# Transposing the attention probabilities by a DMA through DRAM in an attention and MLP kernel

## The chip, the cores and the metric

The kernel runs on one core of one Trainium2 chip. A core has TensorE (PE in the profile; PEld is its weight load), VectorE (DVE), ScalarE (ACT), GpSimd (POOL) and SyncE (SP), each with an instruction queue of its own that is worked through in order, an on-chip memory SBUF of 128 partitions, and the accumulation memory PSUM. Transfers are issued by SyncE and ScalarE and run on 16 DMA engines. The metric is device time in microseconds (us) for one execution, the median of several runs. Before the change it is 1058.22 us over three runs (1056.92 to 1058.27).

## The reference

Attention with a sliding window and a few global tokens, and then a two-layer MLP. Cut to what matters:

```python
# batch 8, heads 8, 512 local and 32 global tokens, head size 64, window 32
s_g  = scale * q_g @ k_all.T                        # 32 global queries see all 544 keys
out_g = softmax(s_g) @ v_all
s_ll = where(|i - j| <= 32, scale * q_l @ k_l.T, -1e9)
s_lg = scale * q_l @ k_g.T
a_l  = softmax(concat([s_lg, s_ll]))                # local queries: 32 global keys and the band
out_l = a_l @ concat([v_g, v_l])
x = concat([out_g, out_l]) as (4608 tokens, 512)
h = x @ w_in                                        # 512 -> 2048
result = (h * sigmoid(h)) @ w_out                   # 2048 -> 512
```

All is float32. The softmax divides by its sum plus 1e-9.

## The kernel before

The work is laid out as 128 attention steps (k = 0 to 127), each for one batch element, 128 local queries and a pair of heads (u = 0, 1), and as an MLP over 12 blocks of tokens (the first of 128 tokens, the rest of 384). For each block and each of 16 slices of the hidden layer, `first_layer` runs 12 matmuls (L600) and an activation chain over ScalarE and VectorE (L606, L608, L612, L613), and `second_layer` runs three matmuls for each 128 tokens (L628 to L630). Float32 accuracy comes from products of high and low parts: a tensor is rounded to the one-pass type `fp32r` (`hi`), and the rest is kept as `lo`.

The order on TensorE is the order of the program, written out by hand: every part of an attention step is put on a stream with a due time, counted in steps, and `fill` advances that stream as MLP matmuls are issued. The due times of the parts stand in `DUE`: `load=-1.2, split=-0.5, vload=-0.6, vsplit=0.95, turn=1.6, out=2.2`, relative to the step's scores. The order on the other engines and on the DMA queues is made by a planner that simulates the program; each engine then keeps to that order.

One step from k = 16 on goes like this. `st_load` and `st_vload` fetch queries with keys (`raw`) and values (`vraw`). `st_split` and `st_vsplit` make high and low parts (L320 to L322, L330, L331). `st_scores` runs the score matmuls (L350), adds the mask with a row minimum on VectorE (L354), takes the exponential on ScalarE (L358), and divides by the sum: head 0 on ScalarE (L362), head 1 on VectorE (L363). The probabilities, [128 queries, 2 heads, 256 columns, of which 224 are used] in float32, lie in `probs`. A DMA on SyncE's queue (L370) copies them to `rr`, a tile of type `fp32r`. `st_turn` transposes `rr` in four blocks of 128 x 128 on TensorE into the PSUM tile `t` (L385), ScalarE rounds `t` to `pt_hi` (L406), and VectorE makes `pt_lo` (L407); GpSimd puts the global part beside it (L409, L410). `st_out` multiplies by the values (L452 with `pt_hi`, L454 with `pt_lo`), and the results go by way of `xs` (L460, L461) into the MLP's input `xh`, `xl` (L462, L463) and into the sum `acc` (L465, L467). `pt_hi` and `pt_lo` are single tiles, so the turn of a step waits for the output matmuls of the step before. Steps below k = 16 transpose `probs` itself in full float32 (L383).

Weights are unpacked and split in the first sixth of the run (`join_weights`, `split_weights`; L211 is the split's part on GpSimd).

Of the kernel before, what the change touches and what calls it, by code (L numbers as in the profile page):

```python
# [20 lines left out]
P = 128  # L21
# [3 lines left out]
W = 224  # L25
# [10 lines left out]


SIZES = (1,) + (3,) * 11
BUFS = dict(qk=2, raw=2, p=2, vraw=2, rr=1)
ND = 28  # L40
KF = 16
GF = 3
KP = 12
# [6 lines left out]
             gload=(1.2, 2.2, 3.2, 3.3), gscores=(3.4, 4.2, 5.1, 6.0), gsoft=(4.4, 6.2), gturn=(6.9, 8.0),  # L50
             join=(3.9, 5.0, 5.9, 6.8), late=8.5, then=7.3)

DUE = dict(load=-1.2, split=-0.5, vload=-0.6, vsplit=0.95, turn=1.6, out=2.2)
HEAD = dict(load=-0.2, split=0.45, scores=0.65, soft=0.85, slot=0.3)
HEADS0, HEADS = (10, 1), (7, 2)
TURN = (1.15, 2.15)
# [4 lines left out]
def attention_moe_kernel(ctx: ExitStack, tc: tile.TileContext, qk0_in, qk_in, v_in, gqk, wts, out):  # L61
    nc = tc.nc

    const = ctx.enter_context(tc.tile_pool(name="const", bufs=1))
    raws = ctx.enter_context(tc.tile_pool(name="raws", bufs=BUFS["raw"]))
    work = ctx.enter_context(tc.tile_pool(name="work", bufs=1))
    two = ctx.enter_context(tc.tile_pool(name="two", bufs=2))
    small = ctx.enter_context(tc.tile_pool(name="small", bufs=4))
    ps_att = ctx.enter_context(tc.tile_pool(name="ps_att", bufs=1, space=PSUM))
    ps_h = ctx.enter_context(tc.tile_pool(name="ps_h", bufs=2, space=PSUM))  # L70
    ps_out = ctx.enter_context(tc.tile_pool(name="ps_out", bufs=1, space=PSUM))
# [19 lines left out]
    ident = const.tile([P, P], F32R, name="ident")  # L91
# [16 lines left out]
    mask_of = [masks[0]] + [masks[1]] * (NC - 2) + [masks[2]]  # L108
# [6 lines left out]
        return const.tile([P, 2 * DM], dtype, tag=f"wh{i}", name=name)  # L115


    probs = [const.tile([P, 2, 2 * P], F32, name=f"probs{i}") for i in range(BUFS["p"])]
    more = [scratch(SCRATCH - 1 - i, F32, f"probs{i}_") for i in range(2)]
    probs += [more[i // 2][:, DM * (i % 2) : DM * (i % 2 + 1)].rearrange("p (u j) -> p u j", u=2) for i in range(3)]  # L120
    for t in probs:
        nc.gpsimd.memset(t, 0.0)
    pgs = [const.tile([P, SKV], F32, name=f"pg{i}") for i in range(2)]

    pts = []
# [9 lines left out]
        return work.tile([P, 2, 2, P + SG], F32, tag="pt_lo" if k % 2 else "pt_hi", name=f"pt{k}")  # L135

    def probs_tile(k):
        i = k % (len(probs) if k < KP else BUFS["p"])
        held_by[i] = k
        return probs[i]  # L140

    held_by = {}

# [14 lines left out]
    def qk_tiles(name):  # L158
        return (work.tile([P, QW + KW], F32R, tag="qk", bufs=BUFS["qk"], name=f"qk{name}"),
                work.tile([P, SKV], F32R, tag="klo", bufs=BUFS["qk"], name=f"klo{name}"))  # L160

    def rr_tile(k):
        return work.tile([P, 4 * P], F32R, tag="rr", bufs=BUFS["rr"], name=f"rr{k}")

    w_32, w_hi, w_lo, w_raw, w_next = [], [], [], [], [0, 0]
# [11 lines left out]
    def join_weights():  # L179
# [81 lines left out]
    def g_soft(b, hh):  # L261
# [32 lines left out]
    tiles = {}  # L294
# [40 lines left out]
    def st_scores(k, b, c, pr):  # L335
        if k < ND:
            raw = tiles.pop(("raw", k))
        else:
            qk, klo = tiles.pop(("qk", k))
        s = attbank("s", f"s{k}")  # L340
        for u in range(2):
            o = s[:, u * W : (u + 1) * W]
            qs = slice(u * P, (u + 1) * P)
            if k < ND:
                terms = [(raw[:, qs], raw[:, QW : QW + W])]
            else:
                ks = slice(u * W, (u + 1) * W)
                terms = [(qk[:, qs], qk[:, QW:][:, ks]), (qk[:, qs], klo[:, ks])]
            for i, (q, kt) in enumerate(terms):
                nc.tensor.matmul(o, q, kt, start=(i == 0), stop=(i == len(terms) - 1))  # L350
        p = probs_tile(k)
        st = small.tile([P, 8], F32, tag="st", name=f"st{k}")
        for u in range(2):
            nc.vector.tensor_tensor_reduce(out=p[:, u, :W], in0=s[:, u * W : (u + 1) * W], in1=mask_of[c],  # L354
                                           scale=-SCALE, scalar=3.0e38, op0=ALU.add, op1=ALU.min,
                                           accum_out=st[:, u : u + 1])
        for u in range(2):
            nc.scalar.activation(p[:, u, :W], p[:, u, :W], AF.Exp, bias=st[:, u : u + 1], scale=-1.0,  # L358
                                 accum_out=st[:, 2 + u : 3 + u])
        nc.vector.tensor_scalar(out=st[:, 4:6], in0=st[:, 2:4], scalar1=1e-9, scalar2=None, op0=ALU.add)  # L360
        nc.vector.reciprocal(out=st[:, 6:8], in_=st[:, 4:6])
        nc.scalar.activation(p[:, 0, :W], p[:, 0, :W], AF.Copy, scale=st[:, 6:7])  # L362
        nc.vector.tensor_scalar(out=p[:, 1, :W], in0=p[:, 1, :W], scalar1=st[:, 7:8], scalar2=None,  # L363
                                op0=ALU.mult)
        if k < KF:
            tiles["p", k] = p.rearrange("p u j -> p (u j)")
            return

        rr = rr_tile(k)
        nc.sync.dma_start(out=rr.bitcast(F32), in_=p.rearrange("p u j -> p (u j)"))  # L370
        tiles["rr", k] = rr

    def st_turn(k, b, c, pr):
        whole = k < KF
        t = attbank("t", f"t{k}")
        if whole:
            p = tiles.pop(("p", k))
            assert k in held_by.values()
        else:
            rr = tiles.pop(("rr", k))  # L380
        for i in range(4):
            if whole:
                nc.tensor.transpose(t[:, i * P : (i + 1) * P], p[:, i * P : (i + 1) * P], ident.bitcast(F32))  # L383
                continue
            nc.tensor.transpose(t[:, i * P : (i + 1) * P].bitcast(F32R), rr[:, i * P : (i + 1) * P], ident)  # L385
        t4 = t.rearrange("p (u a q) -> p u a q", u=2, a=2)
        if k < NPR:

            pt = tiles["pt", k] = pt_whole(k)
            nc.scalar.copy(out=pt[:, :, :, :P], in_=t4)  # L390
            return
        did(("last", b) if (c, pr) == (NC - 1, NPR - 1) else k, ("turn", b, pr // 2))
        pgt, pgh, pgl = state["pgt"]
        g = pgt[:, c, 2 * pr : 2 * pr + 2, :]
        if whole:
            pt = tiles["pt", k] = pt_whole(k)
            nc.scalar.copy(out=pt[:, :, :, :P], in_=t4)
            nc.gpsimd.tensor_copy(out=pt[:, :, 0, P:], in_=g)
            if c == NC - 1:
                rows = slice(SG * pr, SG * (pr + 1))  # L400
                hi, lo = (part.bitcast(F32)[rows, :].rearrange("p (u q) -> p u q", u=2) for part in (pgh, pgl))
                nc.gpsimd.memset(pt[:, :, 1, P:], 0.0)
                nc.gpsimd.tensor_tensor(out=pt[:SG, :, 1, P:], in0=hi, in1=lo, op=ALU.add)
            return
        pt_hi, pt_lo = pt_tiles(k)
        nc.scalar.copy(out=pt_hi[:, :, :, :P], in_=t4)  # L406
        nc.vector.tensor_tensor(out=pt_lo[:, :, :, :P], in0=t4, in1=pt_hi[:, :, :, :P].bitcast(F32),  # L407
                                op=ALU.subtract)
        nc.gpsimd.tensor_copy(out=pt_hi[:, :, 0, P:], in_=g)  # L409
        nc.gpsimd.tensor_tensor(out=pt_lo[:, :, 0, P:], in0=g, in1=pt_hi[:, :, 0, P:].bitcast(F32),  # L410
                                op=ALU.subtract)
        if c == NC - 1:
            for pt, part in ((pt_hi, pgh), (pt_lo, pgl)):
                src = part[SG * pr : SG * (pr + 1), :].rearrange("p (u q) -> p u q", u=2)
                nc.gpsimd.tensor_copy(out=pt[:SG, :, 1, P:], in_=src)
# [99 lines left out]
    for k, (t, b, c, pr) in enumerate(steps):  # L515
        a = (k, b, c, pr)
        j = k % NST
# [47 lines left out]
    ends, t = [], 0  # L565
# [168 lines left out]
```

## Time and profile before

| | |
|---|---|
| runs | 1056.92, 1058.27, 1058.22 us, median 1058.22 |
| span of the profiled execution | 1057.0 us, mean granted TensorE clock 0.993 |
| TensorE busy | 1024.4 us (97%), 6128 matmuls |
| VectorE, ScalarE, GpSimd busy | 757.8 (72%), 732.6 (69%), 187.4 us (18%) |
| DMA | 126.01 MB, mean 119 GB/s; 33.1% of the 16 engines' time on SyncE's queue |
| `rr` | 112 transfers of 256 KB, 2.3 us from issue to landing |

The profiled execution is one execution; its span, from the first to the last instruction, is all the page has of its time, and lies within the times of the runs. In the rows, a group of instructions is named by line, engine and operation, then output and inputs; `x448` is their number, and behind the bar stand the busy time in us and the mean length of one in ns. Matmuls overlap, so what one costs is the distance from its start to the next one's start, not its length. In a timeline row the first number is the start in us, the second the length.

### The profile page before, as it was taken

To read this page: it belongs to the slowest core of one execution; us is meant where nothing else is said; L and a number is where in the kernel's file an instruction comes from. 1 tells how busy PE (TensorE), PEld (TensorE's weight loads), DVE (VectorE), ACT (ScalarE), POOL (GpSimd) and SP (SyncE) were. 2 spreads that over 40 slices of the span, in tenths; PEclk is the share of its full clock that TensorE was granted. 3 is DMA by queue.
4 is the path that set the end of the run, shared out by engine and by line. 5 is a ranking of instruction groups with operands and counts; after the bars stand their busy time and mean duration, and the time that the engine had idled before them with its cause. 6 is when DMAs were issued, how large, how long until landed. Compare 5 with 4: busy or idle time off the path is not lost.

```text
span 1057.0 us, 19736 instructions
## 1 busy us (share of the span) xinstructions
PE 1024.4 (97%) x6128; PEld 915.2 (87%) x6128; DVE 757.8 (72%) x2297; ACT 732.6 (69%) x1965; POOL 187.4 (18%) x480
## 2 busy tenths in 40 slices
PE   6898989999999999999999999999999999999998
PEld 4666878899898898899998898899999989999996
DVE  4877747787788878876668887887887877664322
ACT  6778867777786777776568777777777877654322
POOL 2015755111111111111001111111111111110000
PEclk8999999999999999999999999999999999999999
DMA  8894222433343343442234334344333433300000
GB/s 300 289 345 153 91 76 82 159 115 98 113 148 122 112 135 110 126 129 74 82 96 145 100 113 134 120 126 134 114 115 112 141 115 115 114 34 20 31 1 31
DMA packets 67305, 126.01 MB, mean 119 GB/s; under 512 B 7552, under 2 KB 27520, under 8 KB 67200
## 3 DMA queue, kind: packets, MB, share of 16 engines
q1 hardware_dynamic: 63456, 111.11, 33.1%
q10 hardware_dynamic: 3744, 13.63, 3.6%
q8 instruction: 49, 0.80, 0.3%
q14 instruction: 56, 0.46, 0.1%
HBM read 86.44 MB, written 8.91 MB: 90 GB/s over the span
## 4 chain that ended last, share of the span: by engine, by line
PE 78%; DVE 9%; ACT 8%; issue 3%; DMA 2%; SPq 1%; POOL 0%; ACTq 0%; DVEq 0%
PE h L600 31%; PE out L628 10%; PE out L630 10%; PE out L629 10%; PE s L350 5%; PE o L452 4%; PE o L454 3%; PE t L385 3%; ACT probs L358 2%; DVE pt_lo L407 1%; ACT t L606 1%; PE gs L245 1%; DVE w L200 1%; DVE t L608 1%; ACT w_hi L210 1%
## 5 line engine op out<-in xcount | busy, mean ns | idle before, releaser
L600 PE MATMUL h<-xh,w_hi 128*128 128x384 f32 x704 | 240.6, 342 | 0.0
L600 PE MATMUL h<-xl,w_hi 128*128 128x384 f32 x704 | 238.2, 338 | 0.0
L600 PE MATMUL h<-xh,w_lo 128*128 128x384 f32 x704 | 237.8, 338 | 0.0
L628 PE MATMUL out<-w_hi,gh 128*128 128x512 f32 x528 | 219.2, 415 | 0.0
L630 PE MATMUL out<-w_hi,gl 128*128 128x512 f32 x528 | 209.0, 396 | 0.3 <-DVE gl L613 0.3
L629 PE MATMUL out<-w_lo,gh 128*128 128x512 f32 x528 | 208.2, 394 | 0.0
L606 ACT ACTIVATE t<-h 128x384 f32<-128x384 f32 (+1 forms) x192 | 90.7, 472 | 146.6 <-PE h L600 139.8
L608 DVE SCALAR_TENSOR_TENSOR t<-t,h 128x384 f32<-128x384 f32 x176 | 97.2, 552 | 103.5 <-ACT t L606 102.2
L600 PEld LDWEIGHTS h<-xl,w_hi 128*128 128x128 f32 x704 | 132.5, 188 | 6.0 <-DVE xl L463 0.7
L600 PEld LDWEIGHTS h<-xh,w_hi 128*128 128x128 f32 x704 | 132.5, 188 | 5.2
L600 PEld LDWEIGHTS h<-xh,w_lo 128*128 128x128 f32 x704 | 132.3, 188 | 0.0
L613 DVE TENSOR_TENSOR gl<-t,gh 128x384 fp32r<-128x384 f32 x176 | 100.4, 570 | 43.0 <-PE out L630 39.0
L358 ACT ACTIVATE probs<-probs,st 128x224 f32<-128x224 f32 x244 | 115.7, 476 | 14.4 <-DVE st L354 13.3
L630 PEld LDWEIGHTS out<-w_hi,gl 128*128 128x128 f32 x528 | 99.5, 188 | 23.8 <-DVE gl L613 0.7
L409 POOL CAST pt_hi<-pgt 128x64 fp32r<-128x64 f32 x112 | 34.7, 310 | 473.8 <-PE o L454 336.1
L354 DVE CUSTOM_DVE_ANT_0 probs<-s,mask 128x224 f32<-128x224 f32 x244 | 85.4, 385 | 38.0 <-PE s L350 32.8
L628 PEld LDWEIGHTS out<-w_hi,gh 128*128 128x128 f32 x528 | 99.9, 189 | 12.4 <-issue 1.7
L629 PEld LDWEIGHTS out<-w_lo,gh 128*128 128x128 f32 x528 | 100.3, 190 | 10.8
L612 ACT CAST gh<-t 128x384 fp32r<-128x384 f32 x176 | 89.9, 511 | 26.1 <-DVE t L608 22.6
L452 PE MATMUL o<-pt_hi,vv 128*128 128x160 f32 x448 | 89.1, 266 | 2.6 <-DVE pg L251 1.7
L461 DVE TENSOR_TENSOR xs<-o,xs 64x160 f32<-64x160 f32 x224 | 70.6, 315 | 28.1 <-ACT xs L460 23.8
L452 PEld LDWEIGHTS o<-pt_hi,vv 128*128 128x128 f32 x448 | 82.5, 189 | 9.2 <-issue 5.3
(120 smaller groups left out, 1850.9 us busy)
## 6 DMA issues: line engine op xcount, KB each, us to landing
raw<-in_qk_dram SPq DMA_DIRECT2D x100, 352.0 KB, 3.0
rr<-probs SPq DMA_DIRECT2D x112, 256.0 KB, 2.3
vraw<-in_v_dram SPq DMA_DIRECT2D x128, 128.0 KB, 2.3
raw_w<-in_wts_dram ACTq DMA_DIRECT2D x26, 512.0 KB, 6.3
raw_g<-in_gqk_dram SPq DMA_DIRECT2D x32, 304.0 KB, 2.8
out_dram<-o SPq DMA_DIRECT2D x31, 256.0 KB, 2.5
raw<-in_qk_dram SPq DMA_DIRECT2D x28, 240.0 KB, 4.2
raw_w<-in_wts_dram SPq DMA_DIRECT2D x6, 512.0 KB, 7.0
```

The source lines that it names most:

```text
L354: nc.vector.tensor_tensor_reduce(out=p[:, u, :W], in0=s[:, u * W : (u + 1) * W], in1=mask_of[c], scale=-SCALE, scalar=3.0e38, op0=ALU.add, ...
L358: nc.scalar.activation(p[:, u, :W], p[:, u, :W], AF.Exp, bias=st[:, u : u + 1], scale=-1.0, accum_out=st[:, 2 + u : 3 + u])
L452: nc.tensor.matmul(o[:, at], vv[:, a, u].rearrange("p t d -> p (t d)"), pt_hi[:, u, a, :m], start=(a == 0), stop=(a == 1))
L461: nc.vector.tensor_tensor(out=xs[rows, :], in0=o[:D, at], in1=xs[rows, :], op=ALU.add)
L600: nc.tensor.matmul(h[:, :nt], wt, x[:, c, :nt], start=(i == 0), stop=(i == 3 * NCC - 1))
L606: nc.scalar.activation(t[:, :nt], h[:, :nt], AF.Tanh, scale=0.5)
L608: nc.vector.scalar_tensor_tensor(out=out[:, :nt], in0=t[:, :nt], scalar=1.0, in1=h[:, :nt], op0=ALU.add, op1=ALU.mult)
L612: nc.scalar.copy(out=gh[:, :nt], in_=t[:, :nt])
L613: nc.vector.tensor_tensor(out=gl[:, :nt], in0=t[:, :nt], in1=gh[:, :nt].bitcast(F32), op=ALU.subtract)
L628: nc.tensor.matmul(o, gh[:, sl], wh, start=(f == 0), stop=False)
L629: nc.tensor.matmul(o, gh[:, sl], wl, start=False, stop=False)
L630: nc.tensor.matmul(o, gl[:, sl], wh, start=False, stop=(f == NF - 1))
```

## The change

For steps from k = 16 on, the probabilities are seen as 16 bit halves. GpSimd copies each head's into a tile `halves`, low and high halves apart; a DMA writes `halves` into a DRAM tile `away` (two of them in turn); a transposing DMA reads `away` as a matrix of 256 rows (query, half) by 512 columns and writes its transpose into the SBUF tile `turned`, which read as float32 is the transposed probabilities. `pt_hi` and `pt_lo` are then made from `turned` instead of from the PSUM tile. The TensorE transposes of these steps, `rr` and its DMA are gone. The probabilities of these steps rotate over three half tiles instead of two whole ones, `vraw` has one buffer instead of two, and three due times move: `vload` from -0.6 to 0.2, `turn` from 1.6 to 1.7, `out` from 2.2 to 2.4. For the steps below k = 16 the tiles named `halves` and `turned` serve as probability tiles.

```diff
-BUFS = dict(qk=2, raw=2, p=2, vraw=2, rr=1)
+BUFS = dict(qk=2, raw=2, p=2, vraw=1)
...
-DUE = dict(load=-1.2, split=-0.5, vload=-0.6, vsplit=0.95, turn=1.6, out=2.2)
+DUE = dict(load=-1.2, split=-0.5, vload=0.2, vsplit=0.95, turn=1.7, out=2.4)
...
+    planes = ctx.enter_context(tc.tile_pool(name="planes", bufs=2, space=bass.MemoryType.DRAM))
...
-    probs = [const.tile([P, 2, 2 * P], F32, name=f"probs{i}") for i in range(BUFS["p"])]
+    probs = [const.tile([P, 2, 2 * P], F32, name="probs0")]
+    probs += [work.tile([P, 2, 2 * P], F32, tag=tag, name=f"probs_{tag}") for tag in ("turned", "halves")]
...
-    for t in probs:
+    third = const.tile([P, 2 * P], F32, name="third")
+    for t in probs + [third]:
         nc.gpsimd.memset(t, 0.0)
+    heads = [probs[0][:, 0], probs[0][:, 1], third]
...
     def probs_tile(k):
-        i = k % (len(probs) if k < KP else BUFS["p"])
+        if k >= KF:
+            return [heads[(2 * (k - KF) + u) % 3] for u in range(2)]
+        i = k % (len(probs) - 1 if k < KP else BUFS["p"])
         held_by[i] = k
-        return probs[i]
+        return [probs[i][:, u] for u in range(2)]
...
         if k < KF:
-            tiles["p", k] = p.rearrange("p u j -> p (u j)")
+            tiles["p", k] = p
             return
-
-        rr = rr_tile(k)
-        nc.sync.dma_start(out=rr.bitcast(F32), in_=p.rearrange("p u j -> p (u j)"))
-        tiles["rr", k] = rr
+        halves = work.tile([P, 2, 2, 2 * P], U16, tag="halves", name=f"halves{k}")
+        for u in range(2):
+            nc.gpsimd.tensor_copy(out=halves[:, :, u], in_=p[u].bitcast(U16).rearrange("p (j h) -> p h j", h=2))
+        away = planes.tile([P, 2, 4 * P], U16, tag="away", name=f"away{k}")
+        nc.sync.dma_start(out=away, in_=halves.rearrange("p h u j -> p h (u j)"))
+        turned = work.tile([P, 4, 2 * P], U16, tag="turned", name=f"turned{k}")
+        nc.sync.dma_start_transpose(out=turned, in_=away.rearrange("q h j -> (q h) j"))
+        tiles["turned", k] = turned
...
         else:
-            rr = tiles.pop(("rr", k))
-        for i in range(4):
-            if whole:
-                nc.tensor.transpose(t[:, i * P : (i + 1) * P], p[:, i * P : (i + 1) * P], ident.bitcast(F32))
-                continue
-            nc.tensor.transpose(t[:, i * P : (i + 1) * P].bitcast(F32R), rr[:, i * P : (i + 1) * P], ident)
-        t4 = t.rearrange("p (u a q) -> p u a q", u=2, a=2)
+            t4 = tiles.pop(("turned", k)).bitcast(F32).rearrange("p (u a) q -> p u a q", u=2)
```

More of the change, by code (lines that the diff above doesn't have):

```diff
@@ L14 @@
 U32 = mybir.dt.uint32
+U16 = mybir.dt.uint16
 AF = mybir.ActivationFunctionType
@@ L160, in qk_tiles @@
                 work.tile([P, SKV], F32R, tag="klo", bufs=BUFS["qk"], name=f"klo{name}"))
-    def rr_tile(k):
-        return work.tile([P, 4 * P], F32R, tag="rr", bufs=BUFS["rr"], name=f"rr{k}")
     w_32, w_hi, w_lo, w_raw, w_next = [], [], [], [], [0, 0]
@@ L353, in st_scores @@
         for u in range(2):
-            nc.vector.tensor_tensor_reduce(out=p[:, u, :W], in0=s[:, u * W : (u + 1) * W], in1=mask_of[c],
+            nc.vector.tensor_tensor_reduce(out=p[u][:, :W], in0=s[:, u * W : (u + 1) * W], in1=mask_of[c],
                                            scale=-SCALE, scalar=3.0e38, op0=ALU.add, op1=ALU.min,
@@ L357, in st_scores @@
         for u in range(2):
-            nc.scalar.activation(p[:, u, :W], p[:, u, :W], AF.Exp, bias=st[:, u : u + 1], scale=-1.0,
+            nc.scalar.activation(p[u][:, :W], p[u][:, :W], AF.Exp, bias=st[:, u : u + 1], scale=-1.0,
                                  accum_out=st[:, 2 + u : 3 + u])
@@ L361, in st_scores @@
         nc.vector.reciprocal(out=st[:, 6:8], in_=st[:, 4:6])
-        nc.scalar.activation(p[:, 0, :W], p[:, 0, :W], AF.Copy, scale=st[:, 6:7])
-        nc.vector.tensor_scalar(out=p[:, 1, :W], in0=p[:, 1, :W], scalar1=st[:, 7:8], scalar2=None,
-                                op0=ALU.mult)
+        nc.scalar.activation(p[0][:, :W], p[0][:, :W], AF.Copy, scale=st[:, 6:7])
+        nc.vector.tensor_scalar(out=p[1][:, :W], in0=p[1][:, :W], scalar1=st[:, 7:8], scalar2=None, op0=ALU.mult)
         if k < KF:
-            tiles["p", k] = p.rearrange("p u j -> p (u j)")
+            tiles["p", k] = p
             return
-        rr = rr_tile(k)
-        nc.sync.dma_start(out=rr.bitcast(F32), in_=p.rearrange("p u j -> p (u j)"))
-        tiles["rr", k] = rr
+        halves = work.tile([P, 2, 2, 2 * P], U16, tag="halves", name=f"halves{k}")
[6 more added lines that the diff above has]
+        tiles["turned", k] = turned
     def st_turn(k, b, c, pr):
         whole = k < KF
-        t = attbank("t", f"t{k}")
         if whole:
+            t = attbank("t", f"t{k}")
             p = tiles.pop(("p", k))
             assert k in held_by.values()
-        else:
-            rr = tiles.pop(("rr", k))
-        for i in range(4):
-            if whole:
-                nc.tensor.transpose(t[:, i * P : (i + 1) * P], p[:, i * P : (i + 1) * P], ident.bitcast(F32))
-                continue
-            nc.tensor.transpose(t[:, i * P : (i + 1) * P].bitcast(F32R), rr[:, i * P : (i + 1) * P], ident)
-        t4 = t.rearrange("p (u a q) -> p u a q", u=2, a=2)
+            for i in range(4):
+                nc.tensor.transpose(t[:, i * P : (i + 1) * P], p[i // 2][:, P * (i % 2) : P * (i % 2 + 1)],
+                                    ident.bitcast(F32))
+            t4 = t.rearrange("p (u a q) -> p u a q", u=2, a=2)
+        else:
+            t4 = tiles.pop(("turned", k)).bitcast(F32).rearrange("p (u a) q -> p u a q", u=2)
         if k < NPR:
```

## The prediction

> **What bounds the kernel now.** I read the page first (busy time, the forty slices, the chain that ended last), then a window of the middle of the run, then TensorE's timeline around one transposition.
>
> ```profile
> span 1057.0 us, 19736 instructions
> ...
> PE 1024.4 (97%) x6128; PEld 915.2 (87%) x6128; DVE 757.8 (72%) x2297; ACT 732.6 (69%) x1965; POOL 187.4 (18%) x480
> ...
> PE   6898989999999999999999999999999999999998
> ...
> PEclk8999999999999999999999999999999999999999
> ...
> PE 78%; DVE 9%; ACT 8%; issue 3%; DMA 2%; SPq 1%; POOL 0%; ACTq 0%; DVEq 0%
> ```
>
> ```profile
> core 0: us, PE busy (x) PEld busy (x) DVE busy (x) ACT busy (x) POOL busy (x), PEclk, DMA share, GB/s
> 700.00:800.00 100.00, 99.76 (x621) 91.52 (x621) 81.85 (x253) 76.01 (x208) 15.96 (x50) 1.00 0.38 119
> ```
>
> TensorE bounds it: full in nearly every slice, at full granted clock, and on 78% of the chain. VectorE (81.85 us of 100) is the next. What leaves TensorE's order is worth its full time, as long as nothing makes TensorE wait instead.
>
> **What the change removes.** 112 steps (k = 16 to 127) lose four transposes each.
>
> ```profile
> L385 PE MATMUL t<-ident,rr 128*128 128x128 f32 x448 | 51.4, 238 | 0.4 <-ACT pgt L285 0.2 <-DMA rr<-probs 0.2
> ```
>
> ```profile
> 635.38 0.39 PE L630 MATMUL out<-w_hi,gl 128*128 128x512 f32 x1
> 635.61 0.46 PE L385 MATMUL t<-ident,rr 128*128 128x128 f32 x4
> 635.90 0.47 PE L628 MATMUL out<-w_hi,gh 128*128 128x512 f32 x1
> 636.20 0.40 PE L629 MATMUL out<-w_lo,gh 128*128 128x512 f32 x1
> 636.43 0.40 PE L630 MATMUL out<-w_hi,gl 128*128 128x512 f32 x1
> ```
>
> Durations overlap here, so the price is read from starts. From L630 (635.38) to the second matmul behind the transposes (636.20) pass 0.82 us; two starts of this kind lie 0.23 us apart elsewhere (636.20 to 636.43), which makes 0.46. The four transposes cost 0.36 to 0.37 us; the 86 clean places of this form agree within 0.01. 112 x 0.37 = 41.4 us off the bound. That is also the most this change can give.
>
> **What it adds: a longer way from probabilities to output.** Nothing new is on TensorE, so the question is whether the output matmuls (L452) still find `pt_hi` and `pt_lo` ready. Two steps, one ordinary (k = 84) and one close behind its neighbours (k = 75):
>
> ```profile
> 624.53 0.27 PE L350 MATMUL s<-qk 128*128 128x224 f32 x1
> ...
> 628.67 0.48 ACT L362 ACTIVATE probs<-probs,st 128x224 f32<-128x224 f32 x1 [0.18 <-DVE st L361]
> ...
> 628.96 0.37 DVE L363 TENSOR_SCALAR probs<-probs,st 128x224 f32<-128x224 f32 x1
> ...
> 629.72 0.47 SPq L370 DMA_DIRECT2D rr<-probs  x1
> ...
> 631.64 0.27 PE L350 MATMUL s<-qk 128*128 128x224 f32 x1
> ...
> 636.69 0.59 ACT L406 CAST pt_hi<-t 128x512 fp32r<-128x512 f32 x1
> ...
> 637.31 0.69 DVE L407 TENSOR_TENSOR pt_lo<-t,pt_hi 128x512 fp32r<-128x512 f32 x1 [0.29 <-ACT pt_hi L406]
> ...
> 640.62 0.24 PE L452 MATMUL o<-pt_hi,vv 128*128 128x160 f32 x1
> ```
>
> ```profile
> 559.33 0.31 PE L350 MATMUL s<-qk 128*128 128x224 f32 x1
> ...
> 565.02 0.48 ACT L362 ACTIVATE probs<-probs,st 128x224 f32<-128x224 f32 x1 [0.90 <-DVE st L361]
> ...
> 573.80 0.24 PE L452 MATMUL o<-pt_hi,vv 128*128 128x160 f32 x1
> ```
>
> Room: k = 84 has its probabilities at 629.33 and its first output matmul at 640.62, 11.3 us later. The due time of `out` goes from 2.2 to 2.4 steps, worth 0.2 x 7.1 us (631.64 - 624.53) = 1.4; 2.4 steps without transposes pass 0.9 us sooner. That leaves 11.8 us. For k = 75, 573.80 - 565.50 = 8.3, so with the same corrections 8.8 us. I did this for every step up to k = 123 (108 of them): median 11.6; 11 have under 9 us, 15 under 10, 43 under 11, 65 under 12.
>
> Need, piece by piece, with these rows:
>
> ```profile
> 634.93 0.24 POOL L409 CAST pt_hi<-pgt 128x64 fp32r<-128x64 f32 x1 [5.73 <-PE o L454]
> ...
> 637.08 0.21 POOL L465 COPY acc<-xs 128x32 f32<-128x32 f32 x1 [1.51 <-DVE xs L461]
> ```
>
> ```profile
> raw<-in_qk_dram SPq DMA_DIRECT2D x100, 352.0 KB, 3.0
> rr<-probs SPq DMA_DIRECT2D x112, 256.0 KB, 2.3
> vraw<-in_v_dram SPq DMA_DIRECT2D x128, 128.0 KB, 2.3
> raw_w<-in_wts_dram ACTq DMA_DIRECT2D x26, 512.0 KB, 6.3
> ...
> out_dram<-o SPq DMA_DIRECT2D x31, 256.0 KB, 2.5
> ```
>
> - Two GpSimd copies into `halves`, 512 16-bit elements a partition each. 64 elements take 0.24 us, 32 take 0.21, so 0.84 ns an element and 0.62 us a copy: 1.24 (bounds 0.5 and 1.3 a copy, a memset and a two-input pass over 512, shown below). 112 x 1.24 = 139 us more on GpSimd, which is busy 18%.
> - SyncE wakes and issues `away`: 0.4, as `rr` does now (629.33 to 629.72). Landing in DRAM: 2.5, the row of `out_dram`, same bytes and direction.
> - The transposing DMA waits for that landing, 0.1. Its landing is shown nowhere in this trace. Nearest rows: at the low end 2.3 (`rr`, same bytes), at the high end 6.3 (512 KB of weights). I take 3.0, the row of `raw`, a DRAM to SBUF load by the same queue of somewhat more bytes.
> - ScalarE's turn comes 0.4 later; L406 and L407 take 1.31 from start to end now (636.69 to 638.00), and read SBUF in place of PSUM, taken alike; 0.1 to TensorE.
>
> Sum 9.05 us, and 0.4 for the port below: 9.45 us. The ordinary step keeps 2 us; 14 of the 108 fall short. A step that is e late delays TensorE by e, and by that much the steps in flight behind it gain room, so I replayed the 108 rooms in order, pushing everything behind a late one. The total stall: 4 us for a need of 8.5, 8 at 9.05, 12 at 9.45, 19 at 10, 42 at 11.1, 83 at 12.75, 162 at 15.65. **Taken: +12 us.**
>
> **The port of VectorE and GpSimd.**
>
> ```profile
> 102.44 1.13 DVE L363 TENSOR_SCALAR probs<-probs,st 128x224 f32<-128x224 f32 x1
> ```
>
> ```profile
> 99.55 3.88 POOL L211 TENSOR_TENSOR w_lo<-w,w_hi 128x512 fp32r<-128x512 f32 x3
> 103.38 0.28 POOL L409 CAST pt_hi<-pgt 128x64 fp32r<-128x64 f32 x1
> ```
>
> ```profile
> L211 POOL TENSOR_TENSOR w_lo<-w,w_hi 128x512 fp32r<-128x512 f32 x32 | 41.8, 1324 | 13.6 <-ACT w_hi L210 13.4
> ...
> L122 POOL MEMSET probs<- 128x512 f32 x2 | 1.0, 524 | 0.0
> ```
>
> L363, 0.37 us elsewhere, took 1.13 and ended 0.14 us behind GpSimd's third L211 (103.43): it waited for GpSimd's instruction to end. [...] So each copy may hold up VectorE by at most its own 0.62 us, 1.24 us a step. I take half, 0.6: VectorE's 81.85 us in a window of 14 steps become 90, against 95 that TensorE then needs. TensorE stays the bound with little room left on VectorE. The MLP's own chain has slack today:
>
> ```profile
> DVE gl L613 <- PE out L630: 39.0, 47, 3.1
> ...
> DVE probs L354 <- POOL mask L104: 4.1, 1, 4.1
> ```
>
> VectorE waits for TensorE there, not the reverse. So the loss is between 0 and the whole gain (a rival below); near the first: **+4 us**.
>
> **Edits with one answer.** `rr` and its copy go (0.47 us of SyncE's time, off the path). SyncE now stands at the transposing DMA for `away` to land, some 2.5 us a step, with the loads behind it: `raw` is due 0.7 of a step, 5 us, ahead of its split, and `vraw`, now single and due 0.2 instead of -0.6, is issued at the latest when SyncE is free again, 2.5 us behind the next scores (probabilities 4.8, copies and wake 1.7, landing 2.5, issue 0.6, less 7.1), and lands 2.3 later, at 4.8, for a split due at 0.95 x 7.1 = 6.7. If the transposing DMA is slow, that cover goes first, and ScalarE stands at L330 with the MLP's work behind it. `turned` and `halves` are single: each is free again a few us before the next step's turn. The added memsets (0.52 for a tile, 0.31 for `third`) may stand before the mask for which the first L354 waits: 0 to 0.83, taken 0.4.
>
> **Sum:** 1057.0 - 41.4 + 12 + 4 + 0.4 = 1032 for the profiled execution; the median of the runs, 1058.22, lies 1.2 above its span, so 1033.
>
> **Rivals.**
> 1. Nothing stalls: need under 8.5 us, the transposing DMA like `rr`, stall 4 at most and VectorE's idle time absorbs the port. 1058 - 41 + 1 = 1018. For it: `rr`'s 2.3. Against: 11 steps have under 9 us.
> 2. Slower: the transposing DMA is late and TensorE waits at L452. With the other pieces as above, the gain is gone when it takes 4.4 us (need 10.9, stall 37, beside the 4 us of the port); at the 6.3 us of the 512 KB load the need is 12.75, stall 83, time 1058 - 41 + 83 + 4 = 1104. For it: it scatters 131,072 two-byte elements, and no row has such a pattern. Against: the engines are far from full (0.38 of their time in the window).
>    A sharper form: it goes by 128-column blocks, four in a row at `rr`'s 2.3, 9.2 us, need 15.65, stall 162, time 1183. [...]
> 3. VectorE becomes the bound: every copy blocks it for its full time. 81.85 + 14 x 1.24 = 99.2 us where the window had 100. The gain shrinks to about 1%, and with TensorE's waits behind an engine with no idle time left, to nothing: 1050 to 1058. For it: the 1.13 us row. Against: it takes VectorE to meet every copy for its whole length, and VectorE is idle 18 us of that window's 100.
>
> **How the numbers follow.** The forecast's own case (1020 to 1048) has 0.53; rival 1, 0.12; rival 3, 0.09, of which some 0.05 within 0.2%; rival 2, 0.26, a fifth of it the form by blocks. No change means within 0.2%, 2 us, about what a measurement of this kernel can tell. Faster: 0.53 + 0.12 + 0.03 = 0.68; same 0.05 to 0.06; slower 0.26 to 0.27. The range runs from all of the saving with nothing paid, 1016, into rival 2 up to a need of 12 us (stall 64, 1085), which leaves about 0.15 outside. The likeliest case's own range is 1020 to 1048.
>
> **What would show it.** Right: no L385, TensorE's busy share still 96% or more, stalls before L452 and L454 together near 12 us and only in steps that follow closely; the transposing DMA near 3.0 us to landing; GpSimd near 330 us busy; L363, L613 and L407 some tenths of a us longer on average, VectorE near 88% in the middle slices. Wrong: a transposing DMA over 4.4 us, TensorE waiting at L452 in every step, copies of over 1 us, or ScalarE waiting at L330 or L406 with L606 behind it.

## The result, and the profile after

| | before | after |
|---|---|---|
| median of the runs | 1058.24 us | 1150.16 us (1148.11 to 1155.69) |
| ratio to before, 95% interval | 1 | 1.088 (1.0852 to 1.0907) |
| span, mean granted clock of the profiled execution | 1057.0, 0.993 | 1146.3, 0.965 |

The forecast was 1033 us; the kernel became 92 us slower. The page of the kernel after, the lines that answer to those of before:

```profile
span 1146.3 us, 19145 instructions
PE 1029.8 (90%) x5680; PEld 902.6 (79%) x5680; DVE 776.9 (68%) x2297; ACT 740.4 (65%) x1965; POOL 339.9 (30%) x706
...
PE   6888888889988897989999989897999989999998
...
PEclk8999889999999898899999999998999999999999
...
PE 48%; DMA 24%; DVE 11%; ACT 9%; issue 4%; SPq 1%; POOL 1%; ACTq 0%; DVEq 0%; POOLq 0%
```

```profile
700.00:800.00 100.00, 87.61 (x487) 77.99 (x486) 75.21 (x221) 67.42 (x179) 30.95 (x66) 0.97 0.56 145
```

TensorE issues 448 matmuls fewer and yet is busy longer (1029.8 against 1024.4 us), largely because some run at half the clock (some 80 us of the span against 15; the last section has the records). In the middle window it was full and is now 87.61 busy. VectorE and ScalarE fell too (75 and 67 of 100), so neither took over as the bound. On the chain TensorE fell from 78% to 48%, and DMA rose from 2% to 24%.

The waits of TensorE, ScalarE and SyncE's queue (us in all, times, longest), the group of the rounding on ScalarE, and the new transfers (us from issue to landing):

```profile
PE o L456 <- issue: 24.0, 22, 3.5
PE o L458 <- DVE pt_lo L411: 17.8, 37, 1.0
PE gu L290 <- DVE st L357: 14.2, 9, 2.8
PE gs L251 <- DVE xs L465: 8.7, 6, 2.2
...
ACT pt_hi L410 <- DMA turned<-away: 98.8, 68, 3.4
...
SPq L376 <- DMA away<-halves: 167.7, 72, 4.1
SPq L304 <- DVE qk L325: 164.6, 60, 5.5
...
SPq L314 <- DVE xs L465: 59.3, 24, 5.9
```

```profile
L410 ACT CAST pt_hi<-turned 128x512 fp32r<-128x512 f32 x112 | 69.2, 618 | 100.4 <-DMA turned<-away 98.8
L372 POOL COPY halves<-probs 128x512 uint16<-128x512 uint16 x150 | 100.8, 684 | 100.4 <-DVE probs L366 54.6 <-DMA away<-halves 23.5 <-ACT probs L365 16.4
...
away<-halves SPq DMA_DIRECT2D x112, 256.0 KB, 2.9
...
turned<-away SPq DMA_TRANSPOSE x112, 3.4
```

(In these rows L353, L357, L361, L365, L366, L410, L411, L456, L458 and L465 are L350, L354, L358, L362, L363, L406, L407, L452, L454 and L461 of before. L372, L374, L376 are the copies, the transfer to `away` and the transposing DMA; L304 and L314 are the loads of `raw` and `vraw`. `gs` and `gu` are tiles of the global scores and of their transposition.) The pieces taken one by one, by their medians, are not far from the forecast: 0.61 us a copy (mean 0.68), 2.9 and 3.4 us for the transfers. But ScalarE waits 98.8 us for `turned`, in 68 steps of 112, and SyncE stands 167.7 us for `away` to land. One such step, in time order:

```profile
504.11 0.51 DVE L366 TENSOR_SCALAR probs<-probs,st 128x224 f32<-128x224 f32 x1
504.68 0.61 POOL L372 COPY halves<-probs 128x512 uint16<-128x512 uint16 x1
506.65 0.33 SPq L304 DMA_DIRECT2D raw<-in_qk_dram  x1
507.39 0.33 SPq L314 DMA_DIRECT2D vraw<-in_v_dram  x1
507.76 0.43 SPq L374 DMA_DIRECT2D away<-halves  x1
...
509.08 0.34 PE L604 MATMUL h<-xh,w_lo 128*128 128x384 f32 x1
...
510.85 1.23 SPq L376 DMA_TRANSPOSE turned<-away  x1
...
514.06 0.62 ACT L410 CAST pt_hi<-turned 128x512 fp32r<-128x512 f32 x1 [2.51 <-DMA turned<-away]
514.71 0.69 DVE L411 TENSOR_TENSOR pt_lo<-turned,pt_hi 128x512 fp32r<-128x512 f32 x1 [1.37 <-ACT pt_hi L410]
514.78 0.31 PE L456 MATMUL o<-pt_hi,vv 128*128 128x160 f32 x1 [2.83 <-issue]
...
516.71 0.60 PE L604 MATMUL h<-xh,w_hi 128*128 128x384 f32 x1
```

The copies end at 505.29, but `away` is issued 2.5 us later: two loads stand ahead of it in SyncE's order and wait for their own tiles. Then 3.0 us to landing, 3.2 for the transposing DMA, ScalarE idle for 2.51, TensorE for 2.83, and behind it the matmuls run at half the clock (L604 takes 0.60 us at 516.71, 0.34 at 509.08). From probabilities (504.62) to `pt_lo` (515.40) it takes 10.8 us. Over the 112 steps the mean is 12.1: copies 1.5, on to the issue of `away` 1.3, landing 3.0, on to the issue of the transposing DMA 0.8, landing 3.5, then 0.5 to L410 and 1.5 for L410 and L411. The single steps run from 9.1 to 15.9.

### The profile page after: what moved, and what is told of

The parts are those of the page before. It is cut to its first block, busy times and chain, and to the rows that moved or that the text cites. A ratio compares the mean times of both kernels' runs of the same rounds, so it can differ in the third digit from the quotient of the medians.

```text
span 1146.3 us, 19145 instructions
## 1 busy us (share of the span) xinstructions
PE 1029.8 (90%) x5680; PEld 902.6 (79%) x5680; DVE 776.9 (68%) x2297; ACT 740.4 (65%) x1965; POOL 339.9 (30%) x706
## 4 chain that ended last, share of the span: by engine, by line
PE 48%; DMA 24%; DVE 11%; ACT 9%; issue 4%; SPq 1%; POOL 1%; ACTq 0%; DVEq 0%; POOLq 0%
PE h L604 19%; DMA turned<-away 16%; PE out L632 6%; PE out L634 6%; PE out L633 6%; DMA away<-halves 5%; ACT pt_hi L410 3%; DVE pt_lo L411 3%; PE o L456 2%; PE s L353 2%; PE o L458 2%; ACT probs L361 1%; DVE gl L617 1%; PE gs L248 1%; ACT qk L323 1%
## 5 line engine op out<-in xcount | busy, mean ns | idle before, releaser
L604 PE MATMUL h<-xh,w_hi 128*128 128x384 f32 x704 | 245.4, 349 | 3.2 <-ACT xh L466 3.2
L604 PE MATMUL h<-xl,w_hi 128*128 128x384 f32 x704 | 242.5, 344 | 0.4 <-DVE xl L467 0.3
L604 PE MATMUL h<-xh,w_lo 128*128 128x384 f32 x704 | 241.5, 343 | 0.0
L634 PE MATMUL out<-w_hi,gl 128*128 128x512 f32 x528 | 213.5, 404 | 0.3 <-DVE gl L617 0.3
L633 PE MATMUL out<-w_lo,gh 128*128 128x512 f32 x528 | 212.9, 403 | 0.0
L411 DVE TENSOR_TENSOR pt_lo<-turned,pt_hi 128x512 fp32r<-128x512 f32 x112 | 81.2, 725 | 97.2 <-ACT pt_hi L410 96.5
L604 PEld LDWEIGHTS h<-xh,w_hi 128*128 128x128 f32 x704 | 136.1, 193 | 10.9 <-ACT xh L466 4.2
L604 PEld LDWEIGHTS h<-xl,w_hi 128*128 128x128 f32 x704 | 136.2, 193 | 8.1 <-DVE xl L467 1.5
L617 DVE TENSOR_TENSOR gl<-t,gh 128x384 fp32r<-128x384 f32 x176 | 106.9, 607 | 45.5 <-PE out L634 40.1
L604 PEld LDWEIGHTS h<-xh,w_lo 128*128 128x128 f32 x704 | 135.4, 192 | 0.0
L410 ACT CAST pt_hi<-turned 128x512 fp32r<-128x512 f32 x112 | 69.2, 618 | 100.4 <-DMA turned<-away 98.8
L372 POOL COPY halves<-probs 128x512 uint16<-128x512 uint16 x150 | 100.8, 684 | 100.4 <-DVE probs L366 54.6
L456 PE MATMUL o<-pt_hi,vv 128*128 128x160 f32 x448 | 97.4, 277 | 32.5 <-issue 24.0
L456 PEld LDWEIGHTS o<-pt_hi,vv 128*128 128x128 f32 x448 | 85.4, 195 | 45.6 <-issue 36.3
L458 PE MATMUL o<-pt_lo,vv 128*64 128x160 f32 x448 | 90.0, 241 | 26.3 <-DVE pt_lo L411 17.8
L633 PEld LDWEIGHTS out<-w_lo,gh 128*128 128x128 f32 x528 | 103.3, 196 | 12.8
```

Source lines behind the costliest of these rows:

```text
L372: nc.gpsimd.tensor_copy(out=halves[:, :, u], in_=p[u].bitcast(U16).rearrange("p (j h) -> p h j", h=2))
L456: nc.tensor.matmul(o[:, at], vv[:, a, u].rearrange("p t d -> p (t d)"), pt_hi[:, u, a, :m], start=(a == 0), stop=(a == 1))
L458: nc.tensor.matmul(o[:D, at], vv[:, a, u, 0], pt_lo[:, u, a, :m], start=False, stop=(a == 1), skip_group_check=(a == 1))
L604: nc.tensor.matmul(h[:, :nt], wt, x[:, c, :nt], start=(i == 0), stop=(i == 3 * NCC - 1))
L617: nc.vector.tensor_tensor(out=gl[:, :nt], in0=t[:, :nt], in1=gh[:, :nt].bitcast(F32), op=ALU.subtract)
L633: nc.tensor.matmul(o, gh[:, sl], wl, start=False, stop=False)
```

## The experiments: a ladder from before to after

The result asks where 41 us of saving and 92 more went. Four kernels and the change itself put its parts back one at a time. Steps are ratio differences times 1058.2 us. The planner lays a new order for each kernel, so a step is the price of a part together with the order that it brings; the same part costs another sum beside other parts, as the due times and the fourth half tile show below.

| kernel | median us | ratio (95%) | step |
|---|---|---|---|
| before | 1058.2 | 1 | |
| e15: transposes gone, nothing in their place, old `turn` and `out` (three half tiles and one `vraw`, as after) | 1026.4 | 0.969 (0.9674 to 0.9707) | -33 |
| e14: and the new due times 1.7 and 2.4 | 1055.2 | 0.9966 (0.9953 to 0.9979) | +29 |
| e13: and GpSimd's copies | 1085.2 | 1.0239 (1.0219 to 1.026) | +29 |
| e1: and both transfers, nobody waits for them | 1089.7 | 1.0292 (1.0274 to 1.0311) | +6 |
| after: and `pt_hi`, `pt_lo` made from `turned` | 1150.2 | 1.088 (1.0852 to 1.0907) | +62 |

e1 came first:

```diff
-            t4 = tiles.pop(("turned", k)).bitcast(F32)...
+            t4 = ident.bitcast(F32)...to_broadcast([P, 2, 2, P])
```

> Copies, both DMAs and every queue stay as in the changed kernel; only pt_hi and pt_lo are made from the resident identity tile instead of from turned, so nothing waits for the transposing DMA (this leaves out the use of the probabilities). Theory W (TensorE, ScalarE and VectorE wait in order for turned, because the way from probabilities to pt_lo, 12.1 us on average, is longer than the room of 11.8 us): the waits go, 1058 - 41 and some small stalls, 1016 to 1030 us. Theory P (the added copies and transfers hold VectorE and the queues up, whoever waits for turned): stays above 1100 us.

Measured 1089.68, between the two theories. So waiting for `turned` is worth 62 us, and 72 us above the ideal of 1058 - 41 have nothing to do with it. e13 leaves out the two transfers as well, e14 also the copies, and e15 also takes back two due times:

```diff
-        away = planes.tile(...)
-        nc.sync.dma_start(out=away, ...)
-        turned = work.tile(...)
-        nc.sync.dma_start_transpose(out=turned, ...)
...
-        halves = work.tile(...)
-        for u in range(2):
-            nc.gpsimd.tensor_copy(out=halves[:, :, u], ...)
...
-DUE = dict(..., turn=1.7, out=2.4)
+DUE = dict(..., turn=1.6, out=2.2)
```

> e1's kernel (pt_hi and pt_lo made from the identity tile) without the two transfers of each step; GpSimd's copies into halves stay. e1 took 1089.7. Theory D (the transfers cost by themselves, through SyncE's queue in front of the loads and by halves being held until away has landed): 1045 to 1065. Theory P (the copies and the late row pass cost, by the port that GpSimd and VectorE share): within 8 us of 1090.

> As e13, without GpSimd's copies too: nothing of the new path is left, and TensorE's transposes are gone as well. By e9 the due times cost 20: 1058 - 41 + 20 = 1037. Theory P: most of what e13 leaves above 1037 goes here. If the due times cost more without the transposes between the score and output matmuls: 1050 or more.

> As e14, with the turn and output due times of the kernel before (1.6 and 2.2). If the saving of the prediction (41 us of TensorE) is there once nothing else is in the way: 1015 to 1022. If TensorE's time saved is lost to other waits, nearer 1035.

Measured 1085.23, 1055.18 and 1026.43. The transfers alone, with nobody waiting for them, cost 6: the theory that they disturb the rest falls. The waits of TensorE in e15 and then e14:

```profile
PE gs L251 <- DVE xs L457: 2.1, 3, 1.4
```

```profile
PE gs L251 <- DVE xs L457: 20.7, 12, 2.7
```

With `out` at 2.4 the output matmuls come at phase 0.4 of a step, close before the global scores at 0.65, whose second half takes the same bank of PSUM and waits until `xs` has read it. e9 sets the three due times and the single `vraw` in the kernel before:

```diff
-BUFS = dict(qk=2, raw=2, p=2, vraw=2, rr=1)
+BUFS = dict(qk=2, raw=2, p=2, vraw=1, rr=1)
...
-DUE = dict(load=-1.2, split=-0.5, vload=-0.6, vsplit=0.95, turn=1.6, out=2.2)
+DUE = dict(load=-1.2, split=-0.5, vload=0.2, vsplit=0.95, turn=1.7, out=2.4)
```

> The kernel before, with TensorE's transposes, but with the due times that the change set (turn 1.7, out 2.4, vload 0.2, one buffer for v's raw tile). Nothing else moves. Theory B (a good part of the loss is the moved due times: the output matmuls at 2.4 stand close before the global scores at 0.65, which need the same output bank): 1075 to 1100 us, with TensorE's waits at L251 (kernel after's numbering) for xs as in e1. Theory H (the loss is ScalarE and VectorE standing for the turned tile, and due times alone cost nothing): within 5 us of 1058.

Measured 1078.83, ratio 1.0196 (1.0181 to 1.0211): +21 us for the four settings together. The same wait appears (L248 is L251 of after; the kernel before has no such row):

```profile
PE gs L248 <- DVE xs L461: 10.5, 6, 2.2
```

That the moved due times cost is shown twice; that the bank is the way is read from these rows. A second output bank, the one that the transposes had left free, was tried in the kernel after:

```diff
+        if not early and not spare and kind == "o" and next(banks["o"]) % 2:
+            kind = "t"
```

> The kernel after, with its due times, but the bank of PSUM that the transposes left free from step 17 on is taken for every second output tile (outputs and the second half of the global scores alternate between two banks). Theory B: the waits at L251 and L458 for the output bank go, some 25 to 40 us less, 1110 to 1125. Theory H: the bank is held only because ScalarE stands for the turned tile; the time stays above 1135.

Measured 1148.73, ratio 1.0849 (1.0827 to 1.0871). The waits of L251 for `xs` do leave the list, but TensorE waits as long at the next place:

```profile
PE o L458 <- ACT pt_hi L412: 35.4, 29, 3.6
PE o L460 <- DVE pt_lo L413: 21.8, 44, 1.2
```

(L458 and L460 are L456 and L458 of after.) The first row probably names what after's page calls "issue": the output matmuls wait for `pt_hi`. So a mended bank shows nothing while they do.

**Why the copies cost 29 us.** Nothing waits for `halves` in e13, yet TensorE waits there for the score bank, which `gu` takes and the row pass (L357) frees; in e14 that wait is a tenth. The rows of e13 and of e14:

```profile
PE gu L290 <- DVE st L357: 18.3, 11, 3.5
```

```profile
PE gu L290 <- DVE st L357: 1.8, 5, 0.4
```

VectorE's order in e13:

```profile
405.71 0.39 DVE L357 CUSTOM_DVE_ANT_0 probs<-s,mask 128x224 f32<-128x224 f32 x1 [0.39 <-PE s L353]
406.02 0.08 DVE L357 DVE_READ_ACCUMULATOR2_ANT st<- 128x1 f32 x1
406.14 0.32 DVE L460 TENSOR_TENSOR xs<-o,xs 64x160 f32<-64x160 f32 x1
406.49 0.56 DVE L607 SCALAR_TENSOR_TENSOR t<-t,h 128x384 f32<-128x384 f32 x1
407.04 0.63 DVE L324 TENSOR_TENSOR klo<-raw,qk 128x448 fp32r<-128x448 f32 x1
407.68 0.47 DVE L325 TENSOR_TENSOR qk<-raw,qk 64x256 fp32r<-64x256 f32 x1
408.18 0.39 DVE L357 CUSTOM_DVE_ANT_0 probs<-s,mask 128x224 f32<-128x224 f32 x1
```

Between the two row passes of one step VectorE does 2 us of other work; so in 61 of 112 steps of e13 (5 of e14, 54 of after). The score bank is held all that time. The two passes write two of three half tiles in rotation, and the second of them is free only when GpSimd has copied the step before. On the chip that copy had long ended (in none of 221 passes of e13 less than 0.5 us before, in half of them over 6); but the planner, in laying down the order, had put other work first. e17 is e13 with a fourth half tile (edge masks left out to make place):

```diff
-heads = [probs[0][:, 0], probs[0][:, 1], third]
+heads = [probs[0][:, 0], probs[0][:, 1], third, fourth]
...
-... % 3]
+... % 4]
```

> e13's kernel (no transfers, pt_hi and pt_lo from the identity tile, copies kept) with four half tiles for probabilities instead of three, so that a step's second half never waits, in the order that was laid down, for the copy of the step before. The tables that mask the edges are left out to make place (every chunk uses the first). Theory T (the third half tile, shared by turns, pushes the second row pass behind other work of VectorE): second row pass 0.3 us after the first, 1055 to 1062 as e14. Theory P (the port that the copies share with VectorE): it stays at 1078 or more.

Measured 1065.19, ratio 1.007 (1.0052 to 1.0088). Work between the passes in 1 step, the wait for `gu` 2.1 us:

```profile
PE gu L291 <- DVE st L358: 2.1, 5, 0.6
```

18 of the 29 us were the third half tile, shared while copies read it; without the copies it costs nothing visible, since in e14 the passes stand together. The other 11 stay open (longer instructions of VectorE beside GpSimd's copies among them: `gl<-t,gh` has a mean of 615 ns here, 579 in e14 without copies).

**Room for the transfers.** Later due times: e2 `turn` 2.0 and `out` 2.9 (from k = 4 on, as the change's own due times); from k = 16 on e3 2.6 and 3.5, with `vload`, `vsplit` and the global turn later; e10 2.4 and 3.3, with the global turn a whole step later so that it keeps its phase.

```diff
-... turn=1.7, out=2.4)                                    (e2)
+... turn=2.0, out=2.9)
...
-TURN = (1.15, 2.15)                                       (e3)
+TURN = (1.75, 2.75)
+            due.update(vload=0.85, vsplit=1.6, turn=2.6, out=3.5)
...
-TURN = (1.15, 2.15)                                       (e10)
+TURN = (2.15, 3.15)
+            due.update(vload=0.4, vsplit=1.4, turn=2.4, out=3.3)
```

> The changed kernel with turn due at 2.0 instead of 1.7 and out at 2.9 instead of 2.4 steps: 0.5 step, 3.9 us, more room before the output matmuls. Theory W: room 15.7 us against a need of 12 to 13 us, so most stalls go: 1020 to 1050 us. Theory P: no change, 1140 to 1155 us.

> The changed kernel with, from k = 16 on, vload 0.85, vsplit 1.6, turn 2.6 and out 3.5 (and the turn of the global part 0.6 step later): 1.1 steps, 8.6 us, more room. Theory W: nothing left to wait for at the output matmuls, 1016 to 1035 us, not above the variant with 0.5 step. If ScalarE still stands at pt_hi for the DMA because the planner puts it there too early, 1040 to 1070 us. Theory P: 1140 to 1155 us.

> The kernel after, with later due times for steps 17 on: turn 2.4 and out 3.3 in place of 1.7 and 2.4, v's load and split moved after them (0.4 and 1.4), and the global turn a whole step later (2.15, 3.15) so that it keeps its place between two scores. The turned tile gets 0.7 step (some 5 us) more to arrive. Theory H: the waits for it, some 60 us by e1, fall to under 20, time 1085 to 1105. Theory B on top of it: with the global scores and turns in their own places as before, e3's extra waits at L353 go too, time 1060 to 1085. If the need of 12 us is not what costs: 1130 or more.

Measured 1150.45 (ratio 1.0856), 1128.66 (1.066) and 1111.36 (1.0507; 1.0489 to 1.0524). ScalarE's wait for `turned` in e2, e3 and e10:

```profile
ACT pt_hi L410 <- DMA turned<-away: 70.1, 51, 3.0
```

```profile
ACT pt_hi L410 <- DMA turned<-away: 16.9, 13, 2.9
```

```profile
ACT pt_hi L410 <- DMA turned<-away: 49.6, 35, 3.0
```

The wait shrinks with room, but the time doesn't follow it. In e2 nothing is won at all, against the forecast of theory W. There the output matmuls come 4.6 us behind the end of the rounding (median; 1.5 in the kernel after), so TensorE had its room; but ScalarE still starts the rounding at once when `turned` lands in half of the steps, so it stood there waiting, and TensorE's waits at L251 for `xs` grow to 34.3 us from 8.7. e3 has the least wait of the three and is slower than e10. In e3 the global turn stands just ahead of a step's scores and shares their bank, and the scores wait for it:

```profile
PE s L353 <- DVE pgl L294: 24.5, 12, 3.3
```

Phase and room both seem to count. The fourth half tile (edge masks left out to make place), first alone in e5, then with e3 (e6) and with e10 (e18):

> The changed kernel with four half tiles for the probabilities instead of three, so that a step's second head doesn't wait for the copy of the step before (to make room, all steps use the middle mask: the two edge masks are left out, which changes no instruction on the way). In the changed kernel VectorE's second row pass comes 1.36 us behind the first on average, 0.32 before the change. Theory S (the third half tile shared by two steps holds VectorE up, and with it the score bank and TensorE): this falls back to 0.3 to 0.5 us and the time to 1100 to 1120 us. Theory W alone (the way to pt_lo is too long for the room): the way gets 1 us shorter at most, 1125 to 1140 us. Neither: 1145 to 1155 us.

> Both together: 1.1 steps more room as in the variant that took 1129 us, and four half tiles (edge masks left out). Theory W and S together (room first, then the slots bind): 1030 to 1070 us. If neither is the cause of what remained there: 1115 to 1130 us.

> e10's kernel (0.7 step more room, the global work in its own places) with four half tiles, edge masks left out. In e10 TensorE waits 40 us for the row pass (L290, L251, L248, L353 <- st) and its clock is at half for 60 us. Theory T: these waits go, 1075 to 1090. If they come from elsewhere: 1105 to 1112. Below 1058 only if the remaining waits for the turned tile are hidden too.

Measured 1144.81 (ratio 1.0812), 1117.02 (1.0569) and 1076.71 (1.0189; 1.0157 to 1.0221). The same edit gives 7 us alone and 34 on top of e10: one wait mended shows little while another stands behind it. e18 is the best of the versions with the whole path, still 20 us above before; ScalarE waits 25.4 us for `turned` in it. e12 adds the second output bank to e10 and changes nothing:

> Both: later due times as in e10 and the second output bank as in e11. If H and B together are the whole of the loss, TensorE waits no more than in the kernel before, its clock comes back to 0.99, and the time is 1020 to 1040 us, below the kernel before. If something else costs (the halved clock by itself, the tail of the MLP's activations), it stays at 1050 or more.

Measured 1110.86.

**Who stands.** e16 makes `pt_hi` and `pt_lo` on GpSimd, so that ScalarE and VectorE never stand for `turned`:

```diff
-        nc.scalar.copy(out=pt_hi[:, :, :, :P], in_=t4)
-        nc.vector.tensor_tensor(out=pt_lo[:, :, :, :P], in0=t4, ...
+        nc.gpsimd.tensor_copy(out=pt_hi[:, :, :, :P], in_=t4)
+        nc.gpsimd.tensor_tensor(out=pt_lo[:, :, :, :P], in0=t4, ...
```

> The kernel after, with pt_hi and pt_lo made from the turned tile by GpSimd instead of ScalarE and VectorE, so that those two never stand for the transposing transfer; GpSimd does, and the copies of the next step stand behind it. GpSimd gets some 112 times 2.2 us more, 590 us in all. Theory H (what costs is ScalarE and VectorE standing with the MLP's activations behind): 1090 to 1115. Theory L (the lateness itself costs, wherever the wait stands): the need grows by about 1 us and the copies come later, 1150 to 1200.

Measured 1187.83, ratio 1.1186 (1.1131 to 1.124). TensorE now waits for the late tile directly:

```profile
PE o L458 <- POOL pt_lo L411: 65.7, 43, 5.2
```

Theory H forecast a gain and is not borne out, but e16 doesn't settle it: the two passes take 3.0 us on GpSimd instead of 1.5, the transposing DMA is issued 2.1 us behind the landing of `away` instead of 0.8, and the whole way is 14.7 us instead of 12.1. Where the wait stands and how late the tile is changed together; which of the two costs stays open.

**Smaller ones.** e4 lets GpSimd issue the transfer to `away`; e7 gives `vraw` its second buffer back (edge masks left out); e8 uses the DMA path in odd steps only, and TensorE's transposes in even ones.

```diff
-        nc.sync.dma_start(out=away, ...)                  (e4)
+        nc.gpsimd.dma_start(out=away, ...)
...
-BUFS = dict(qk=2, raw=2, p=2, vraw=1)                     (e7)
+BUFS = dict(qk=2, raw=2, p=2, vraw=2)
...
+        if k % 2 == 0:                                    (e8)
+            rr = work.tile([P, 4 * P], F32R, tag="halves", ...)
+            ...
+            return
```

> The changed kernel with the transfer into away issued by GpSimd right behind its copies instead of by SyncE. Theory Q (the need is long because SyncE's queue has loads standing ahead of away and of the transposing DMA: 1.27 us from copy to issue and 0.82 us from landing to issue on average): about 1.5 us less need, at 25 us of stall per us some 35 us faster, about 1110 to 1120 us. Theory W without Q: within 10 us of 1150. If issuing from GpSimd is itself slow or its order worse: slower than 1150 us.

> The changed kernel with two buffers for vraw again (edge masks left out). Theory Q (SyncE stands at the load of vraw until the step before has split its values, 59 us in all, with away and the transposing DMA behind it in the queue): the wait from copy to issue falls from 1.27 us to about 0.6 and the time by 15 to 30 us, 1120 to 1135 us. Otherwise within 8 us of 1150.

> From k = 16 on only the odd steps go through away and turned; the even ones are copied by a DMA into an fp32r tile in the slot of halves (two transfers of half the size) and transposed on TensorE as before the change. 56 x 0.37 = 20.7 us are saved instead of 41.4. Theory R (a step's way through single halves, away, turned and SyncE's queue takes longer than a step, so each step pushes the next; with two steps of time for each it fits): 1058 - 21 + 5 to 15 = 1042 to 1052 us, faster than before the change. Theory P (each added copy and transfer costs by itself): half of the loss, about 1104 us.

Measured 1169.27 (ratio 1.1066), 1150.40 (1.0868) and 1152.49 (1.0905). Taking `away` from SyncE's queue is worse: from the copies to its issue it takes 1.0 us instead of 1.3, but from its landing to the issue of the transposing DMA 1.8 instead of 0.8, and the whole way is 13.1 us. `vraw`'s second buffer changes neither the time nor the wait before `away` (1.3 us as before). And half as many transposing transfers lose nearly as much as all of them, with 70.8 us of waiting in 40 of 56 steps:

```profile
ACT pt_hi L422 <- DMA turned<-away: 70.8, 40, 3.6
```

e8 is no clean test of the number, though. Its even steps issue two plain transfers into `rr`, so SyncE's queue carries as many as before, and `rr` holds the tile of `halves` until TensorE has transposed it: in the odd steps the copies end 3.1 us behind the probabilities instead of 1.5, and the whole way is 13.4 us. GpSimd's wait for it:

```profile
POOL halves L378 <- PE t L399: 46.5, 27, 5.0
```

That the traffic is not the trouble is shown by e1 against e13 (6 us). That each transfer's place in a fixed order is, is read from the traces; no version here had a shorter wait in the queues and the same place for everything else.

## Why the prediction was wrong, step by step

The forecast was 117 us too low. By the ladder, within rounding, this is 8 of saving that didn't come, 29 of due times, 25 more than the 4 booked for the port (18 of them the third half tile), 6 of transfers and 50 more than the 12 booked for stalls.

- **The saving, 41.4 us.** As a bound right. With nothing in its place the removal gives 33 (e15); TensorE's busy time falls by 37 (1024.4 to 987.1), and the rest went to other waits.
- **The need, 9.45 us, and the stall of 12 from it.** This term was mis-sized: without the 0.4 for the port the sum was 9.05, and 12.1 is measured. Of the 3 us that lacked, 1.6 are SyncE's queue (1.3 and 0.8 us from ready to issued where I had 0.4 and 0.1), 1.0 the two transfers (3.0 and 3.5 where I had 2.5 and 3.0), the rest copies and rounding. I saw that SyncE would stand for `away` with the loads behind it, and asked only what that does to the loads, not what the loads do to the next `away`.
- **The place of the wait.** I counted room up to the output matmuls and gave ScalarE's turn 0.4 us. But the wait stands at ScalarE's rounding, 98.8 us, which in the kernel before came 7.9 us behind the probabilities (median), while the outputs came 11.1 behind. `turned` lands 10.1 us behind them on average. In e2 the outputs have 3.9 us more, and nothing is won.
- **The replay.** Its table, 42 us for 11.1 and 83 for 12.75, makes about 67 for 12.1, beside the 62 of e1 against after. This is at least in part luck: the replay takes one need for all steps, though the single ones ran from 9.1 to 15.9, and by the same table e2, with a way of 12.8 us and 3.9 us more room, should have kept under 8 us of stall.
- **The due times.** I booked `out` at 2.4 as 1.4 us of room and nothing else. With `turn` it cost 29 us (21 in the kernel before, with the two other settings). No step of mine asked what else stands at that phase on the output bank, though the global scores' due time was in the code.
- **The three half tiles.** Put at nothing; 18 us of the copies' 29. In my "edits with one answer" I looked whether `turned` and `halves` come free in time, not `probs`; and the tile was free in time on the chip. What changed was the order on VectorE that the planner laid down.
- **The port, +4.** At most 11 (e17 against e14). No run shows that the two engines share a port, only lengths: in the kernel after, `gl<-t,gh` (L617) takes 555 ns on average with no GpSimd instruction beside it (106 of 176, the longest 560) and 686 with one (70, the longest 1656), while `xs` (L465) takes 314 and 316. Rival 3 falls: VectorE is 68% busy.
- **Rival 2** had the direction, not the cause or the price: the transposing DMA took 3.4 us by the median, and only 9 of 112 took over the 4.4 that it needed (the longest 5.0); its form by blocks falls (3.4 us for the whole transfer, where I had 9.2; no run shows transfers that add up block by block). The time is beyond its 1104, and the range too low at 1085, because the due times and the half tiles were in no case of mine.
- Of the signs named, ScalarE waiting at the rounding showed the failure; TensorE's 90%, 58.8 us of idle time before the two output lines where I had 12, and the clock (0.965 for 0.993) came with it. GpSimd's 340 us was as forecast.

## What to carry to other kernels

What a path through a queue takes depends on its place in that queue (here 2.1 of 12.1 us from ready to issued): count, for each new transfer, what is issued ahead of it and what that waits for, not only its landing time. A moved due time and a smaller rotation of buffers are changes of their own; price each by leaving the new work out and keeping only the move (here +29 us with nothing of the new path running, and +18 with only its copies). When several waits hide one another, a mend of one shows little alone (the fourth half tile 7 us, on top of e10 34), and a ladder that puts the parts back one at a time tells more than taking single parts out. Room must be counted at the engine that waits first, here ScalarE with 98.8 us, and not only at the one that bounds the kernel.

## What the hardware showed

The granted clock is 1.0 or 0.5 in the records of these two kernels, so the mean of 0.965 means half clock for 2 x 0.035 x 1146 = 80 us, 15 before. Two places of the kernel after (columns: us, busy us and instructions of PE, PEld, DVE, ACT, POOL; clock; DMA share; GB/s):

```profile
430.25:433.66 3.41, 1.03 (x5) 0.43 (x3) 2.06 (x6) 3.03 (x7) 0.34 (x1) 1.00 0.75 239
433.66:437.08 3.42, 2.86 (x12) 2.60 (x13) 1.48 (x7) 1.84 (x6) 0.56 (x2) 0.51 0.61 170
...
454.14:457.55 3.41, 1.23 (x8) 0.92 (x6) 3.14 (x10) 3.01 (x10) 1.37 (x2) 1.00 0.38 118
457.55:460.97 3.42, 3.42 (x12) 3.33 (x11) 3.09 (x6) 0.89 (x2) 0.53 (x2) 0.51 0.04 14
460.97:464.38 3.41, 3.41 (x24) 3.10 (x23) 2.15 (x8) 2.11 (x4) 0.33 (x1) 0.99 0.67 185
```

In the clock records of this execution each change lies a whole number of 3.41 us behind the one before; of the 19 drops to half, 13 lasted one such stretch, 5 two, and the last ran to the end. At 454 TensorE's one wait was 2.18 us (for `xs`, at L251), but it was busy 1.23 of 3.41; the next stretch, though full, ran at half clock, 12 matmuls where the one after it has 24. Over the run all 19 drops follow a stretch with TensorE busy 0.08 to 0.52 of it; of 291 stretches at full clock without a drop behind them the lowest is 0.49. Only 4 times does a start of TensorE lie more than 3.41 us behind the one before, so most drops came behind stretches in which it still started matmuls. So by an estimate from these rows a wait of 2 us can cost 1.7 more (half of a full stretch), and twice that where the half clock lasts two stretches; (80 - 15) / 2, at most some 33 us of the kernel after, go this way. The steps of the ladder hold their part of it: in the profiled executions the mean clock is 0.993 in e15, 0.987 in e14, 0.973 in e13 and 0.978 in e1.

The transposing DMA holds SyncE for 1.23 us (median of 112, the longest 2.02; 0.33 to 0.43 for the plain ones in the step shown), and lands 256 KB in 3.4 us, against 2.9 for the plain transfer of the same bytes into DRAM (medians).

In the kernel before, a transposition of 128 x 128 starts 64 ns behind the one ahead of it where its input is `fp32r` (L385, median of 336) and 109 ns in float32 (L383, median of 48); how many passes a type takes is not shown by any run.
